# Turning memory rows with a VectorE block transpose, in a memory-augmented recurrent attention kernel

## The chip, the cores and the metric

The kernel runs on one core of one Trainium2 chip. That core has a matrix engine (TensorE, PE in the profile; its weight loads are listed apart as PEld), three engines for elementwise work (VectorE = DVE, ScalarE = ACT, GpSimd = POOL), a SyncE queue (SP) that issues most transfers, and 16 DMA engines that carry them. The metric is the device time of one execution in microseconds, the median over runs.

## The reference

A pre-normalised block with two halves. The first is attention with a recurrent memory: the 2048 tokens of 640 columns are cut into 64 segments of 32 tokens, and eight memory rows are carried from segment to segment.

```python
mem = mem0
for s in range(n_seg):                                # 64 segments, in order
    xs = x[:, s * seg_len:(s + 1) * seg_len, :].copy()
    h = jnp.concatenate([mem, xs], axis=1)            # 8 + 32 rows
    q = jnp.einsum('btd,dhe->bhte', h, Wq)            # 640 -> 32 heads x 128
    k = jnp.einsum('btd,dhe->bhte', h, Wk)
    v = jnp.einsum('btd,dhe->bhte', h, Wv)
    scores = jnp.einsum('bhqe,bhke->bhqk', q, k) * scale
    scores = jnp.where(mask[None, None], scores, -1000000000.0)
    p = _softmax(scores, axis=-1)
    o = jnp.einsum('bhqk,bhke->bhqe', p, v)
    o = jnp.einsum('bhte,hed->btd', o, Wo)            # back to 640 columns
    mem = o[:, :M, :].copy()                          # first 8 rows: next memory
    outs.append(o[:, M:, :])
```

Here x is the layer-normalised input. Its result is added to the input, normalised again and sent through a feed-forward half (640 to 1728, squared ReLU, back to 640, with biases), which is added once more. All tensors are bf16.

## The kernel before

The four attention weights (5 MB each) are loaded once and stay in SBUF. `wq`, `wk` and `wv` are tiles of 128 partitions with five blocks of 4096 columns: block c holds model columns 128c to 128c+127 on the partitions (`load_w`, L117 to L120, five transfers of 1 MB for each weight, issued on SP). In program order SP gets the first input rows, `wv`, `wq`, `wk`, then `wo` (`load_wo`, L142) and after that the smaller transfers of the steps. `start` (L669) computes the values, queries and keys of the first segment block by block as the weights land, and puts projections of later tokens between.

Then 64 calls of `step` (L380) run, one for each segment. Segments are handled in groups of four (b is the group, sp the place in it). The activations lie turned, model column on the partition, in `hT4[:, c, sp, 0:32]`: slots 0 to 7 hold the memory rows, the others the segment's first 24 tokens (filled ahead, by layer norm L171 and TensorE transposes L180). The last eight tokens of each segment are projected ahead for four segments together (`tail_units`). All projections go through `proj` (L206): for each block c and each of four column groups one matmul with 32 stationary columns and 512 moving columns.

A step projects q, k and v (L206), forms scores and softmax of the memory rows, applies them to the values, multiplies by Wo in `wo_rounds` (L238) and ends as follows. `wo_rounds` leaves in `pw` four groups of 32 partitions: two halves of the heads times two halves `ch` of the 640 output columns. `wo_out` (L241 to L247) copies the upper 64 partitions out with ScalarE (L245) and adds them to the lower 64 with VectorE (L246): the sum `o` has 64 partitions of 320 columns. `mem_to_hT` (L312) turns its memory rows with twenty small matmuls against an identity (L316) into PSUM tile `pm`, and VectorE copies that into `hT4` (L318). Only then can the next step's first projection load its weights, since those are the columns of `hT4`. In the halves `ch`, columns are interleaved in runs of 64 (`wov2`, L229), so that these matmuls can put each column on its partition.

The program order is the order on each engine; nothing reorders it. TensorE gets other work between the last `wo_rounds` matmul and the turn: up to six units of `fill` (L563), each of four to eight matmuls of later tokens' projections or Wo products, and what is left of `fill` after the turn (L567), ahead of the next projection. After the turn VectorE does layer norm work (`mid`, L566) and two transposes (L569, L575).

Results go to a DRAM tile `o_all`, in two stores for each step (`store_main`, L341) and two for each group's tails (L299). The values of tail tokens pass through DRAM as well: `vt_d` is written on L279 and read back by `tails_v_in` (L331), four transfers of 64 KB for each group. Their source is a view with j (four) outermost, then k (eight), then a run of 2 KB; the target is 32 partitions (L335, L338). At the end the feed-forward half runs in four tiles of 512 tokens; it loads `o_all` and the input and adds them in `prep_sum` (L635), which undoes the interleaving.

Of the kernel before, what the change touches and what calls it, by code (L numbers as in the profile page):

```python
# [9 lines left out]
ALU = mybir.AluOpType  # L10
AX = mybir.AxisListType
F32 = mybir.dt.float32
BF16 = mybir.dt.bfloat16
# [3 lines left out]
def kernel(  # L17
# [26 lines left out]
    DH = D // 2  # L44
    NB = S // 128
    NS = S // SEG
    HD = 24
# [28 lines left out]
    wo = wts.tile([128, H, D], BF16)  # L76

    ident = const.tile([128, 128], BF16)
    o_ring = [const.tile([128, DH], BF16, name="o%d" % k) for k in range(5)]
    o0 = o_ring[-1]  # L80
    nc.vector.memset(o0[0:64], 0.0)
    make_identity(nc, ident[:])
    mhalf = const.tile([128, 1], F32)
    nc.vector.memset(mhalf[:], -0.5)
# [22 lines left out]
    for o in o_ring:  # L107
        nc.gpsimd.memset(o[64:128], 0.0)

    ctx.enter_context(tc.manual_schedule(engines=None))  # L110

    def head(p):
# [3 lines left out]

    def load_w(w, src):  # L117
        w2d = src.rearrange("d h e -> d (h e)")
        for c in range(DC):
            nc.sync.dma_start(out=w[:, c * HE:(c + 1) * HE], in_=w2d[c * 128:(c + 1) * 128, :])  # L120

    xts = {}

# [9 lines left out]
        xts["t", g] = xt  # L133

    load_x(0)
    for ch in range(2):
        nc.scalar.dma_start(out=o0[32 * ch:32 * ch + M, :].rearrange("m (c f) -> m c f", f=64),
                            in_=A_mem0[0].rearrange("m (c t f) -> t m c f", t=2, f=64)[ch])
    load_tail_rows(0)
    load_w(wv, A_Wv)  # L140

# [25 lines left out]
    def ln_norm(b):  # L167
        mv, rs = xns[b]
        xn = s1.tile([128, D], BF16, tag="xn", name="xn")
        xt = xts.pop(b)  # L170
        nc.vector.tensor_scalar(out=xn[:], in0=xt[:], scalar1=mv[:, 0:1], scalar2=rs[:, 0:1],  # L171
                                op0=ALU.subtract, op1=ALU.mult)
        xns[b] = xn

    def ln_transpose(b):
# [65 lines left out]
    def wo_out(pw):  # L241
        o = o_ring[0]
        o_ring.append(o_ring.pop(0))
        tmp = s1.tile([128, DH], F32, tag="tk", name="otmp")
        nc.scalar.copy(out=tmp[0:64], in_=pw[64:128, 0:DH])  # L245
        nc.vector.tensor_tensor(out=o[0:64], in0=pw[0:64, 0:DH], in1=tmp[0:64], op=ALU.add)  # L246
        return o  # L247

    fill, late, mid, win = [], [], [], []
# [43 lines left out]
    def wo_tail_units(b):  # L293
        st = {}

        def out():
            o = wo_out(st["ps"])
            dst = o_all[:].rearrange("(b s t) d -> b s t d", s=4, t=SEG)
            for ch in range(2):  # L299
                nc.sync.dma_start(out=dst[b, :, HD:SEG, ch * DH:(ch + 1) * DH], in_=o[32 * ch:32 * ch + 32, :])  # L300

        def unit(k):
            def f():
                if k == 0:
                    st["ps"] = mmtile()
                wo_rounds(lambda p: oTts[b % 2][:, p, :], st["ps"], k * 16 // 10, (k + 1) * 16 // 10)
                if k == 9:
                    late.append(out)
            return f
        return [unit(k) for k in range(10)]  # L310

    def mem_to_hT(o, hT4, sp):  # L312
        pm = chn.tile([128, 512], F32, tag="ch", name="pm")
        for c in range(DC):
            for q in range(4):
                nc.tensor.matmul(pm[32 * q:32 * q + 32, c * M:(c + 1) * M], lhsT=o[:, (2 * c + q % 2) * 32:(2 * c + q % 2 + 1) * 32],  # L316
                                 rhs=ident[:, q // 2 * 32:q // 2 * 32 + M], start=True, stop=True)
        nc.vector.tensor_copy(out=hT4[:, :, sp, 0:M], in_=pm[:, 0:DC * M].rearrange("p (c m) -> p c m", m=M))  # L318

    def tails_in(b, sp, which="qk", h0=0, h1=H):  # L320
        q, k = [tails[b][w][:].rearrange("p h (k s) -> p h s k", s=4)[:, h0:h1, sp, :] if w in which else None for w in "qk"]
# [16 lines left out]
            eng.dma_start(out=vt4s[b][32 * g:32 * g + 32].rearrange("p s u e -> p (s u e)")[:, f0:f1], in_=src[g, :, :, f0:f1])  # L338

    def store_main(o, s):  # L340
        for ch in range(2):  # L341
# [392 lines left out]
    for b in range(NB):  # L734
        for sp in range(4):
# [40 lines left out]
            e = b * 4 + sp - (NS - 7)  # L776
# [30 lines left out]
    for t in range(S // NT):  # L807
# [6 lines left out]
        for fc in range(FC):  # L814
            ps = mmtile()
            for c in range(DC):
                if fc < FFULL:
                    nc.tensor.matmul(ps[:], lhsT=w1[:, c, fc * 128:(fc + 1) * 128], rhs=hnT[:, c, :],  # L818
                                     start=(c == 0), stop=(c == DC - 1))
                    continue  # L820
                for hh in range(2):
                    nc.tensor.matmul(ps[FREM * hh:FREM * (hh + 1), 0:HT], lhsT=w1[:, c, fc * 128:F],
                                     rhs=hnT[:, c, HT * hh:HT * (hh + 1)], start=(c == 0), stop=(c == DC - 1))
            w = NT if fc < FFULL else HT
# [3 lines left out]
            if more and fc >= 1 and (fc - 1) // 3 < NK4:  # L828
                k, stage = divmod(fc - 1, 3)
# [10 lines left out]
        for q in range(NK4):  # L840
# [6 lines left out]
            for hh in range(2):  # L847
                k = pr + 2 * hh
# [3 lines left out]
                if more and q and (hh == 0 or q == 1):  # L852
                    k = q if hh == 0 and q > 1 else hh
# [45 lines left out]
```

## Time and profile before

| | |
|---|---|
| median of 3 runs | 1021.12 us (1020.16 to 1023.35) |
| the profiled execution | 1020.98 us, span 1018.8 us |
| PE busy | 972.1 us (95%) |
| DVE busy | 621.6 us (61%) |
| ACT busy | 533.8 us (52%) |
| POOL busy | 309.3 us (30%) |
| HBM read, written | 38.37 MB, 9.44 MB |
| mean granted TensorE clock | 0.996 |

The span runs from the first to the last instruction; the execution's time is 2.2 us longer. An engine's busy time is the union of its instructions, so overlapping ones count once. Idle time is put down to whatever the engine waited for last. The share of the DMA engines is a mean over all 16: at 1.00 all carry packets, and packets that overlap on one engine can take it slightly over.

### The profile page before, as it was taken

The page shows a single profiled execution, that of the slowest core. Times are in us where ns is not written, and L with a number is a line of the kernel's source. Part 1 is how long each engine was busy: PE and PEld are TensorE (multiplying, and loading weights), DVE is VectorE, ACT ScalarE, POOL GpSimd, SP SyncE. Part 2 cuts the span into 40 slices and gives each one's busy share as a digit, 9 for nine tenths or more (in the row PEclk, how much of TensorE's full clock was granted, in tenths as well). Part 3 has the DMA queues.
Part 4 walks back from the last instruction along what each step waited for, and adds up shares of the span by engine and source line. Part 5 has one row for each costly group of instructions (what it writes and reads, how often), then busy time and mean ns, then how long its engine had stood idle before and what let it go on. Part 6 is the DMA issues. An engine that isn't in the chain of part 4 may idle for free.

```text
span 1018.8 us, 58958 instructions
## 1 busy us (share of the span) xinstructions
PE 972.1 (95%) x26951; PEld 582.4 (57%) x26960; DVE 621.6 (61%) x1740; ACT 533.8 (52%) x1229; POOL 309.3 (30%) x803
## 2 busy tenths in 40 slices
PE   5789899999999999999999999999999998999998
PEld 2345555655655755656655666556566565555565
DVE  2256676767666667566667666666666676466432
ACT  3335555565555555555555555555555555533431
POOL 2023333333333333323333332323232343433210
PEclk9999999999999999999999999999999999999999
DMA  9960101000101010000000000000000110612200
GB/s 362 398 190 21 23 7 30 8 24 7 35 7 30 7 38 11 27 10 27 15 21 16 24 19 15 22 14 28 15 22 8 48 35 6 212 48 66 78 26 26
DMA packets 39112, 51.57 MB, mean 51 GB/s; under 512 B 5968, under 2 KB 35024, under 8 KB 36944
## 3 DMA queue, kind: packets, MB, share of 16 engines
q1 hardware_dynamic: 38080, 47.48, 14.1%
q8 instruction: 210, 3.44, 1.4%
q10 hardware_dynamic: 784, 0.34, 0.1%
q14 instruction: 38, 0.31, 0.1%
HBM read 38.37 MB, written 9.44 MB: 47 GB/s over the span
## 4 chain that ended last, share of the span: by engine, by line
PE 88%; DMA 6%; DVE 2%; issue 1%; ACT 1%; SPq 0%; DVEq 0%; POOL 0%; ACTq 0%; POOLq 0%
PE ps L206 48%; PE pw L238 15%; PE y L850 6%; PE ps L818 5%; PE ps L238 3%; DMA wk<-in_A_Wk_dram 3%; PE po L449 2%; PE po L355 2%; PE sm L421 2%; DMA wq<-in_B_w_dram 1%; DMA xt<-in_A_x_dram 1%; PE ps L493 1%; PE pm L316 1%; PE ps L489 1%; DVE o L246 1%
## 5 line engine op out<-in xcount | busy, mean ns | idle before, releaser
L206 PEld LDWEIGHTS <-hT 128*32 128x32 bf16 x7680 | 200.9, 97 | 171.6 <-issue 14.2
L238 PE MATMUL pw<-wo,oT 128*32 128x320 bf16 x4224 | 184.1, 300 | 7.1 <-issue 5.4
L206 PE MATMUL ps<-wv,hT 128*32 128x512 bf16 x2520 | 170.5, 379 | 0.9 <-ACT v L502 0.7
L206 PE MATMUL ps<-wq,hT 128*32 128x512 bf16 x2520 | 160.2, 381 | 5.3 <-DVE hT L318 5.3
L206 PE MATMUL ps<-wk,hT 128*32 128x512 bf16 x2520 | 159.5, 380 | 0.1
L238 PEld LDWEIGHTS <-oT 128*32 128x32 bf16 x4224 | 104.6, 96 | 60.5 <-ACT oT L215 13.6
L222 ACT ACTIVATE row<-ps 128x512 bf16<-128x512 f32 x156 | 93.3, 599 | 75.7 <-PE ps L206 75.1
L227 DVE STREAM_TRANSPOSE qT<-row 128x512 bf16<-128x512 bf16 x128 | 90.4, 707 | 65.8 <-ACT row L222 65.7
L548 POOL TENSOR_TENSOR pkt<-ek,rk 128x64 bf16<-128x64 bf16 x64 | 18.8, 294 | 352.5 <-DVE rk L546 352.5
L224 ACT CAST row<-ps 128x512 bf16<-128x512 f32 x115 | 68.0, 591 | 32.7 <-PE ps L206 32.5
L374 POOL COPY qz<-qT 128x96 bf16<-128x96 bf16 x126 | 33.4, 265 | 139.6 <-DVE qT L227 139.4
L325 POOL COPY kT<-kTt 128x1024 bf16<-128x1024 bf16 (+1 forms) x65 | 71.9, 1107 | 12.5 <-DVE kTt L227 12.5
L206 PEld LDWEIGHTS <-hTt 128*32 128x32 bf16 x1920 | 55.0, 97 | 32.3 <-issue 3.7
L245 ACT COPY otmp<-pw 64x320 f32<-64x320 f32 x66 | 27.9, 423 | 81.8 <-PE pw L238 81.8
L544 DVE TENSOR_REDUCE zk<-ek 128x8 f32<-128x320 bf16 x64 | 31.1, 486 | 63.5 <-ACT ek L542 63.5
L365 ACT CAST oT<-po 128x512 bf16<-128x512 f32 x128 | 68.7, 589 | 1.6
L246 DVE TENSOR_TENSOR o<-pw,otmp 64x320 bf16<-64x320 f32 x66 | 31.8, 482 | 61.6 <-ACT otmp L245 61.6
L227 DVE STREAM_TRANSPOSE kT<-row 128x512 bf16<-128x512 bf16 x65 | 46.1, 709 | 31.3 <-ACT row L224 31.3
L850 PE MATMUL y<-wq,wk 128*128 128x320 bf16 x416 | 60.9, 299 | 0.0
L405 ACT CAST row<-ps 128x256 bf16<-128x256 f32 x126 | 40.7, 375 | 31.2 <-PE ps L206 29.4
L521 ACT CAST v<-ps 128x512 bf16<-128x512 f32 x63 | 36.9, 586 | 30.7 <-PE ps L206 30.7
L502 ACT CAST v<-ps 128x512 bf16<-128x512 f32 x63 | 36.9, 586 | 30.0 <-PE ps L206 30.0
(113 smaller groups left out, 1633.6 us busy)
## 6 DMA issues: line engine op xcount, KB each, us to landing
wv<-in_A_Wv_dram SPq DMA_DIRECT2D x5, 1024.0 KB
wq<-in_A_Wq_dram SPq DMA_DIRECT2D x5, 1024.0 KB
wk<-in_A_Wk_dram SPq DMA_DIRECT2D x5, 1024.0 KB
vt<-vt_d SPq DMA_DIRECT2D x60, 64.0 KB
xt<-in_A_x_dram SPq DMA_DIRECT2D x20, 160.0 KB
vt_d<-row SPq DMA_DIRECT2D x22, 128.0 KB
wo<-in_A_Wo_dram SPq DMA_DIRECT2D x2, 1280.0 KB
wo<-in_A_Wo_dram SPq DMA_DIRECT2D x4, 640.0 KB
```

The source lines that it names most:

```text
L206: nc.tensor.matmul(ps[32 * k:32 * k + 32, :], lhsT=lhs(c), rhs=wr[:, c, n, k], start=(c == 0), stop=(c == DC - 1))
L222: nc.scalar.mul(out=row, in_=ps, mul=scale)
L224: nc.scalar.copy(out=row, in_=ps)
L227: nc.vector.transpose(out=dst[:, n * 16:(n + 1) * 16, 0:32], in_=row.rearrange("p (h e) -> p h e", e=32))
L238: nc.tensor.matmul(pw[32 * j:32 * j + 32, 0:DH], lhsT=lhs(p), rhs=wov2[:, head(p), ch], start=(h == 0), stop=(h == 15))
L246: nc.vector.tensor_tensor(out=o[0:64], in0=pw[0:64, 0:DH], in1=tmp[0:64], op=ALU.add)
L325: nc.gpsimd.tensor_copy(out=kT[:, h0:h1, SEG:2 * SEG].rearrange("p h (j k) -> p h j k", k=TL), in_=k.unsqueeze(2).to_broadcast([128, h1 - ...
L365: nc.scalar.copy(out=oTg[:, n, :, :, M:NK], in_=po[:, :, n * 128:(n + 1) * 128].rearrange("p g (j q) -> p g j q", q=32))
L405: nc.scalar.copy(out=row[:, u * 256:(u + 1) * 256], in_=ps[:, u * 256:(u + 1) * 256])
L502: nc.scalar.copy(out=v[:, 0:512], in_=ps0[:])
L818: nc.tensor.matmul(ps[:], lhsT=w1[:, c, fc * 128:(fc + 1) * 128], rhs=hnT[:, c, :], start=(c == 0), stop=(c == DC - 1))
L850: nc.tensor.matmul(y[:, hh, 0:DH], lhsT=f1T[:, fc, k * 128:(k + 1) * 128], rhs=w2[:, fc, cs], start=(fc == 0), stop=False, skip_group_chec ...
```

## The change

The eight memory rows are turned by one VectorE instruction that transposes each 32x32 block of a 128x160 tile, and one VectorE copy into `hT4`. The twenty matmuls and the PSUM tile `pm` go. For that, `o` becomes 128 partitions of 160 columns: partition group q (of 32) holds model columns 160q to 160q+159. A block transpose then leaves model column 160q + 32c + f on partition 32q + f of block c. So block c of the turned activations holds four runs of 32 model columns, 160 apart, instead of 128 consecutive ones.

Everything that shares this contraction follows: the three weights are loaded with rows in that order (`load_w`: the source of each 1 MB transfer is four runs of 32 rows), the layer norm writes its columns in that order, and the Wo columns are interleaved in runs of 160. `wo_out` makes `o` in two copies and two adds of 64x160 instead of one of each of 64x320. Every store of `o` becomes four transfers of 160 columns instead of two of 320, and so does the load of the first memory rows. `prep_sum` adds plainly, and the clearing of the `o` tiles' upper halves goes.

```diff
     def load_w(w, src):
         w2d = src.rearrange("d h e -> d (h e)")
+        rows = w2d.rearrange("(q c f) e -> c q f e", q=4, c=DC)
         for c in range(DC):
-            nc.sync.dma_start(out=w[:, c * HE:(c + 1) * HE], in_=w2d[c * 128:(c + 1) * 128, :])
+            nc.sync.dma_start(out=w[:, c * HE:(c + 1) * HE], in_=rows[c])
...
-    for ch in range(2):
-        nc.scalar.dma_start(out=o0[32 * ch:32 * ch + M, :].rearrange("m (c f) -> m c f", f=64),
-                            in_=A_mem0[0].rearrange("m (c t f) -> t m c f", t=2, f=64)[ch])
+    for q in range(4):
+        nc.scalar.dma_start(out=o0[32 * q:32 * q + M, :], in_=A_mem0[0][:, q * DQ:(q + 1) * DQ])
...
-        nc.vector.tensor_scalar(out=xn[:], in0=xt[:], scalar1=mv[:, 0:1], scalar2=rs[:, 0:1],
-                                op0=ALU.subtract, op1=ALU.mult)
+        nc.vector.tensor_scalar(out=xn[:].rearrange("p (c q f) -> p c q f", c=DC, q=4),
+                                in0=xt[:].rearrange("p (q c f) -> p c q f", c=DC, q=4),
+                                scalar1=mv[:, 0:1], scalar2=rs[:, 0:1], op0=ALU.subtract, op1=ALU.mult)
...
-    wov2 = wo[:].rearrange("p h (c t f) -> p h t c f", t=2, f=64)
+    wov2 = wo[:].rearrange("p h (a t f) -> p h t a f", a=2, t=2)
...
-        tmp = s1.tile([128, DH], F32, tag="tk", name="otmp")
-        nc.scalar.copy(out=tmp[0:64], in_=pw[64:128, 0:DH])
-        nc.vector.tensor_tensor(out=o[0:64], in0=pw[0:64, 0:DH], in1=tmp[0:64], op=ALU.add)
+        tmp = s1.tile([128, DH], F32, tag="otmp", name="otmp")
+        for a in range(2):
+            nc.scalar.copy(out=tmp[0:64, a * DQ:(a + 1) * DQ], in_=pw[64:128, a * DQ:(a + 1) * DQ])
+        for a in range(2):
+            nc.vector.tensor_tensor(out=o[64 * a:64 * a + 64], in0=pw[0:64, a * DQ:(a + 1) * DQ],
+                                    in1=tmp[0:64, a * DQ:(a + 1) * DQ], op=ALU.add)
...
     def mem_to_hT(o, hT4, sp):
-        pm = chn.tile([128, 512], F32, tag="ch", name="pm")
-        for c in range(DC):
-            for q in range(4):
-                nc.tensor.matmul(pm[32 * q:32 * q + 32, c * M:(c + 1) * M], lhsT=o[:, (2 * c + q % 2) * 32:(2 * c + q % 2 + 1) * 32],
-                                 rhs=ident[:, q // 2 * 32:q // 2 * 32 + M], start=True, stop=True)
-        nc.vector.tensor_copy(out=hT4[:, :, sp, 0:M], in_=pm[:, 0:DC * M].rearrange("p (c m) -> p c m", m=M))
+        mt = s1.tile([128, DC, 32], BF16, tag="mt", name="mt")
+        nc.vector.transpose(out=mt[:], in_=o[:].rearrange("p (c f) -> p c f", f=32))
+        nc.vector.tensor_copy(out=hT4[:, :, sp, 0:M], in_=mt[:, :, 0:M])
...
     def store_main(o, s):
-        for ch in range(2):
-            nc.sync.dma_start(out=o_all[s * SEG:s * SEG + HD, ch * DH:(ch + 1) * DH],
-                              in_=o[32 * ch + M:32 * ch + 32, :])
+        for q in range(4):
+            nc.sync.dma_start(out=o_all[s * SEG:s * SEG + HD, q * DQ:(q + 1) * DQ],
+                              in_=o[32 * q + M:32 * q + 32, :])
...
     def prep_sum(t, k, got):
         ot, fx = got
-        fv = fx.rearrange("p (c t f) -> p t c f", t=2, f=64)
-        nc.vector.tensor_tensor(out=fv, in0=ot.rearrange("p (t c f) -> p t c f", t=2, f=64), in1=fv, op=ALU.add)
+        nc.vector.tensor_tensor(out=fx, in0=ot, in1=fx, op=ALU.add)
         return fx
```

More of the change, by code (lines that the diff above doesn't have):

```diff
@@ L44 @@
     DH = D // 2
+    DQ = D // 4
     NB = S // 128
@@ L78 @@
     ident = const.tile([128, 128], BF16)
-    o_ring = [const.tile([128, DH], BF16, name="o%d" % k) for k in range(5)]
+    o_ring = [const.tile([128, DQ], BF16, name="o%d" % k) for k in range(5)]
     o0 = o_ring[-1]
-    nc.vector.memset(o0[0:64], 0.0)
+    nc.vector.memset(o0[:], 0.0)
     make_identity(nc, ident[:])
@@ L105 @@
     oTts = [const.tile([128, H, 32], BF16, name="oTt%d" % k) for k in range(2)]
-    for o in o_ring:
-        nc.gpsimd.memset(o[64:128], 0.0)
     ctx.enter_context(tc.manual_schedule(engines=None))
@@ L298, in out @@
             dst = o_all[:].rearrange("(b s t) d -> b s t d", s=4, t=SEG)
-            for ch in range(2):
-                nc.sync.dma_start(out=dst[b, :, HD:SEG, ch * DH:(ch + 1) * DH], in_=o[32 * ch:32 * ch + 32, :])
+            for q in range(4):
+                nc.sync.dma_start(out=dst[b, :, HD:SEG, q * DQ:(q + 1) * DQ], in_=o[32 * q:32 * q + 32, :])
         def unit(k):
@@ L340, in store_main @@
     def store_main(o, s):
-        for ch in range(2):
-            nc.sync.dma_start(out=o_all[s * SEG:s * SEG + HD, ch * DH:(ch + 1) * DH],
-                              in_=o[32 * ch + M:32 * ch + 32, :])
+        for q in range(4):
+            nc.sync.dma_start(out=o_all[s * SEG:s * SEG + HD, q * DQ:(q + 1) * DQ],
+                              in_=o[32 * q + M:32 * q + 32, :])
     oTg = oT[:].rearrange("p (n g j) q -> p n g j q", n=2, g=G)
```

## The prediction

> **What bounds the kernel now.** I read the page first: busy shares and the chain that ended last.
>
> ```profile
> PE 972.1 (95%) x26951; PEld 582.4 (57%) x26960; DVE 621.6 (61%) x1740; ACT 533.8 (52%) x1229; POOL 309.3 (30%) x803
> ...
> DMA  9960101000101010000000000000000110612200
> ...
> PE 88%; DMA 6%; DVE 2%; issue 1%; ACT 1%; SPq 0%; DVEq 0%; POOL 0%; ACTq 0%; POOLq 0%
> ```
>
> TensorE carries the chain, except for the first slices (25 us each), where the DMA engines are full. The chain in order of time, narrowed to the first 70 us, shows what they do:
>
> ```profile
> 5.74 12.33 DMA xt<-in_A_x_dram
> 18.09 16.74 DMA wk<-in_A_Wk_dram
> 34.85 10.19 DMA wk<-in_A_Wk_dram
> ...
> 45.08 1.92 PE pa L206 x16
> ...
> 61.61 0.35 PE pm L316 x20
> ```
>
> Until 45.04 us the end is set by weight transfers; the last `wk` block frees TensorE at 45.08. So there are two regimes: a load of 45 us bound by transfers, and steps bound by TensorE. For a step I took the timeline of one with full `fill` (columns: start, duration):
>
> ```profile
> 452.49 0.42 ACT L245 COPY otmp<-pw 64x320 f32<-64x320 f32 x1 [1.11 <-PE pw L238]
> 452.95 0.48 DVE L246 TENSOR_TENSOR o<-pw,otmp 64x320 bf16<-64x320 f32 x1 [0.80 <-ACT otmp L245]
> 453.50 0.28 PE L316 MATMUL pm<-ident,o 128*32 128x8 bf16 x20
> 453.63 0.82 PE L206 MATMUL ps<-wk,hTt 128*32 128x512 bf16 x12
> 453.90 0.20 DVE L318 CAST hT<-pm 128x40 bf16<-128x40 f32 x1 [0.47 <-PE pm L316]
> 454.15 0.67 PEld L206 LDWEIGHTS <-hT 128*32 128x32 bf16 x16 [0.19 <-DVE hT L318]
> 454.28 0.82 PE L206 MATMUL ps<-wq,hT 128*32 128x512 bf16 x12
> ```
>
> The twenty turning matmuls hold TensorE for 0.13 us (453.50 to 453.63). The turned rows are ready at 454.10, their weights load at 454.15, the projection starts at 454.28. The waits say how often that is late:
>
> ```profile
> PE ps L206 <- DVE hT L318: 5.3, 15, 0.4
> ```
>
> In 15 steps TensorE stands still for the turned rows, 0.35 us each; in the other 47 `fill` covers them.
>
> Last, the transfers by stretch, with the share of 16 DMA engines and GB/s as the last two columns:
>
> ```profile
> 8.00:40.00 32.00, 25.08 (x418) 12.24 (x422) 4.70 (x10) 12.38 (x21) 2.10 (x8) 1.00 1.02 414
> 168.90:169.70 0.80, 0.80 (x22) 0.42 (x16) 0.33 (x1) 0.44 (x1) 0.80 (x4) 1.00 0.76 202
> 483.30:486.00 2.70, 2.70 (x89) 2.31 (x84) 2.23 (x6) 1.56 (x6) 0.58 (x4) 1.00 0.25 77
> 742.00:745.00 3.00, 3.00 (x96) 1.69 (x92) 2.24 (x6) 1.90 (x6) 1.16 (x5) 1.00 0.25 78
> ```
>
> The first is the weight load: all engines. The second is `load_tail_rows` (source 16 by 8 rows), well spread. The last two are `tails_v_in`, whose source has an outermost axis of four: a quarter of the engines. Four such transfers are in flight together there and still fill only a quarter, so they queue on the same four engines.
>
> **The weight load.** It moves 15 transfers of 1024 KB, 15.73 MB. Before: 15.73 MB / 414 GB/s = 38.0 us. After, each source reads four by 32 rows of 8 KB: outermost axis four, the form of `tails_v_in`. From those rows I expect four of 16 engines for every transfer, the same four each time. One engine carried 414/16 = 25.9 GB/s with these 8 KB rows; four carry 103.5, and 15.73 MB take 152.0 us: +114.0. The nearest rows bound it. Not at all (0) if the form spreads as `load_tail_rows` does; 15.73 MB / 77 GB/s = 204 us (+166) if the rate of the 2 KB rows holds. I take 114, since the packets stay those of the weight load. Nothing covers it: TensorE already waits for these transfers, `start` needs every block in order, and the work that it holds (39 us busy between 4 and 58) is no longer than the load was. Behind the weights in the SP queue are `wo`, the next input rows and `vt`. `wo` spreads over 16 engines, but its part on those four queues behind `wk`, so it ends about as long after the last `wk` block as before (bounds: -1.2 us, the stall at 58.38 that would go, to 0).
>
> [...]
>
> **Off TensorE.** 64 times 20 matmuls and their weight loads go. In the 47 covered steps that is 0.13 us each, -6.1 us, if the turned rows come in time; they are needed by 454.15 then (454.28 less 0.13).
>
> **The new chain in a step**, on the clock of the timeline above. ScalarE: 128x256 takes 375 ns and 128x512 589, so 0.836 ns an element; 160 elements take about 295, and the second of a back-to-back pair begins some 0.19 later. Copies 452.49 to 452.98 (before 452.91). Adds: PSUM reads of 128x40 and 128x128 take 200 and 292 ns, 1.05 ns an element, so 160 elements save 167 of 483: 316. The first runs 452.82 to 453.13, the second ends about 453.40 (before 453.43). Transpose of 128x160: between the rows for 128x64 (245) and 128x256 (424), by line 335: 453.44 to 453.77. Copy of 128x40: 200 as the PSUM row at most, to 454.01; weights from 454.06. That is 0.09 before need, so the covered steps keep their gain, and the 15 others gain about 0.06 each: -0.9. Together -7.0 us.
> Bounds: durations that do not shrink with halves (copies 0.42 after each other, adds 0.48, transpose 0.42) give 454.54: 47 x 0.31 + 15 x 0.5 = +22. Halved ones (0.21, 0.24, transpose 0.245, copy 0.14) give -6.1 and 15 x 0.38 = -5.7 more: -12. I take -7, by the rows on both sides of each size.
>
> **Beside other work.** DVE gets some 0.5 us more a step, ACT 0.07, in steps of 13 us at 61% and 52%: what follows L318 (`mid`, L569, L575) is needed in the next step only; 0. SP issues 128 plus 32 stores more at 0.35 and 0.61 us; it waits 634.7 us on L342 for `o`, which covers them; behind it stand `vt` loads that are read a group later; 0. Layer norm with runs of 32: 20 instructions of 574 ns, at most 668 (the 128x512 row of L827, 534, scaled to 640): 2 us on DVE in idle time; 0. Wo matmuls with runs of 160: same 320 columns, as L850 with unbroken columns takes 299 and L238 300; 0. `prep_sum` unbroken: 16 of about 500 ns beside the feed-forward matmuls; -3 to 0, I take 0. Two more loads of the first memory rows on ACT (1.4 and 0.7 us an issue) and the five clears off POOL lie beside the first weight block, which now lands later; 0. No wait is added on a queue other than DVE's own order.
>
> **Sum**, against the profiled execution: 1020.98 + 114.0 - 7.0 = 1128.0 us. The median is 0.14 above that execution, so the same number holds for it.
>
> **Rivals.** (1) The loads spread: either the form reaches all engines, as 16 by 8 rows do, or each transfer takes another four. Then the load stays at 38 us and only the steps change: 1020.98 - 7 = 1014, faster. For it: 32 rows a piece are more than the eight of `vt`. Against it: a share of 0.25 with four transfers queued. It decides as soon as more than four engines work: at eight the load is 76 us and the time 1052. (2) The chain is late: the vector work doesn't shrink with size, `fill` runs out in every step, +22 instead of -7: 1157. For it: fixed costs show in every short row (245 ns for 64 columns). Against: the pairs of L405 overlap. (3) Four engines at the slower rate of 2 KB rows, with some of it, say half, made up: +140, 1154. Against: packets of 8 KB remain.
>
> **How the numbers follow.** Four shared engines with the chain in time: 0.75, 1128, own range 1118 to 1140. Rival 2: 0.07. Rival 3: 0.08. Rival 1: 0.10, of which 0.09 end at 1014 and 0.01 between. The range, 1116 to 1155, leaves out rival 1 and the far ends of 2 and 3. No change here means within 0.3%, about 3 us, which is what a measurement of this kernel can tell. Faster 0.09, same 0.01, slower 0.90.
>
> **What would show it.** DMA share near 0.25 and about 104 GB/s through the first 155 us; the last wait for `wk` ending near 159 instead of 45; steps 0.1 us shorter on average with no L316; a transpose of about 0.33 us before L318's successor; L206 waiting for it no more than in 15 steps. A share near 1 in the first slices would overthrow the forecast; a wait for the turned rows in every step would be rival 2.

## The result, and the profile after

The changed kernel takes 1137.12 us (median of 4 runs, 1135.06 to 1139.67), against 1020.96 us for the kernel before: a ratio of 1.114, 95% interval 1.1116 to 1.1165. It is slower by 116 us. The forecast was 1128, with its own range 1118 to 1140, and the range over all cases 1116 to 1155. The profiled execution took 1136.06 us, its span 1134.3 us, with a mean granted TensorE clock of 0.956.

First the page of the changed kernel: busy shares, TensorE's granted clock, the DMA engines and their GB/s in slices of 28 us, and the chain that ended last.

```profile
PE 983.5 (87%) x25671; PEld 560.5 (49%) x25680; DVE 654.7 (58%) x1886; ACT 535.6 (47%) x1311; POOL 304.3 (27%) x798
...
PEclk9965659999999999999999999999999999999999
DMA  2222354000000101010001001010000010242200
GB/s 92 109 113 106 123 174 147 16 16 13 22 14 16 28 11 28 8 37 14 20 14 26 25 9 32 8 28 14 25 14 21 24 39 20 84 141 70 71 24 24
...
PE 11%; DVE 1%; issue 0%; ACT 0%; DVEq 0%
```

Where the row of the DMA engines began with `99`, it begins with four slices of `2`, at 92 to 113 GB/s: the weight load now fills the first six slices. TensorE's clock reads 0.5 to 0.7 in the third to sixth of them. The chain of this run can't be used: followed back it breaks off in the feed-forward half, and its shares add up to 12%.

The windows of the changed kernel over the load show the same by stretch (last two columns: share of the 16 DMA engines, GB/s).

```profile
8.00:60.00 52.00, 9.29 (x81) 3.62 (x85) 1.60 (x5) 1.55 (x2) 0.00 (x0) 1.00 0.26 104
60.00:110.00 50.00, 21.67 (x205) 8.23 (x200) 1.13 (x3) 6.97 (x12) 0.79 (x2) 0.58 0.27 110
110.00:165.00 55.00, 15.78 (x164) 6.19 (x160) 2.49 (x4) 4.32 (x8) 1.36 (x6) 0.59 0.41 134
```

The clock of 1.00 in the first of these rows can't be relied on, nor the mean of 0.956 that includes it: the clock records of this trace begin at 64.6 us. Matmuls of 512 columns take 620 to 634 ns (medians by tile) from 8 to 60 us, much as they do from 68 to 112 us, where the clock is 0.50, and 379 ns from 171 to 230 us, where it is 1.00.

What TensorE waits for in the changed kernel (us in total, times, longest):

```profile
PE pa L205 <- DMA wv<-in_A_Wv_dram: 39.4, 5, 8.3
PE pa L205 <- DMA wk<-in_A_Wk_dram: 39.2, 5, 9.7
PE pa L205 <- DMA wq<-in_A_Wq_dram: 28.3, 5, 6.2
PE ps L205 <- DVE hT L317: 17.1, 15, 2.2
...
PE ps L816 <- DVE o L247: 4.1, 1, 4.1
```

All fifteen weight blocks are waited for, 106.9 us in total, where the kernel before waited 5.9 us (its rows are among the experiments). The wait for the turned rows has grown from 5.3 to 17.1 us, but the kernel before also waited for the same chain one instruction earlier, where its turning matmuls needed the adds. At the start of the feed-forward half the wait is 4.1 us, where it was 1.0. These rows of the kernel before are:

```profile
PE pm L316 <- DVE o L246: 6.3, 10, 1.1
...
PE ps L818 <- DVE o L246: 1.0, 1, 1.0
```

The ten waits of the first row fall in ten of the 15 steps, so the chain cost 11.6 us of waiting before and 17.1 us now.

I cut both profiled executions at the same matmuls. The last column says what the prediction had.

| stretch | before, us | after, us | difference | forecast |
|---|---|---|---|---|
| start to the last `wk` block's first matmul | 45.08 | 164.74 | +119.7 | +114.0 |
| to the last Wo matmul of step 0 | 15.45 | 15.00 | -0.4 | -1.2 to 0 |
| steps 1 to 5 | 66.2 | 67.9 | +1.7 | with the next row |
| steps 6 to 62 | 741.15 | 731.41 | -9.7 | -7.0 in all steps |
| last step and feed-forward half | 150.9 | 155.2 | +4.3 | -3 to 0, taken as 0 |
| span | 1018.8 | 1134.3 | +115.5 | +107.0 |

So the load carries the result, as forecast. The smaller rows come close in their sum, but, as the runs show, not for the reasons that I gave, and in part by luck. The timeline of the changed kernel shows this for the step that the prediction showed (step 30; start, duration):

```profile
568.38 0.48 ACT L245 COPY otmp<-pw 64x160 f32<-64x160 f32 x2 [1.00 <-PE pw L237]
...
568.89 0.67 DVE L247 TENSOR_TENSOR o<-pw,otmp 64x160 bf16<-64x160 f32 x2 [0.76 <-ACT otmp L245]
...
569.59 0.34 DVE L316 STREAM_TRANSPOSE mt<-o 128x160 bf16<-128x160 bf16 x1
...
569.97 0.18 DVE L317 COPY hT<-mt 128x40 bf16<-128x40 bf16 x1
...
570.20 0.34 PEld L205 LDWEIGHTS <-hT 128*32 128x32 bf16 x12 [0.42 <-DVE hT L317]
```

From the first copy to the weights' load it takes 1.82 us (568.38 to 570.20), where the kernel before took 1.66 (452.49 to 454.15) with its twenty matmuls in between.

### The profile page after: what moved, and what is told of

Read it like the earlier page. It is cut to its first block, busy times and chain, and to the rows that moved or that the text cites. A ratio compares the mean times of both kernels' runs of the same rounds, so it can differ in the third digit from the quotient of the medians.

```text
span 1134.3 us, 57176 instructions
## 1 busy us (share of the span) xinstructions
PE 983.5 (87%) x25671; PEld 560.5 (49%) x25680; DVE 654.7 (58%) x1886; ACT 535.6 (47%) x1311; POOL 304.3 (27%) x798
## 5 line engine op out<-in xcount | busy, mean ns | idle before, releaser
L205 PEld LDWEIGHTS <-hT 128*32 128x32 bf16 x7680 | 190.0, 97 | 306.9 <-issue 120.5
L237 PE MATMUL pw<-wo,oT 128*32 128x320 bf16 x4224 | 179.1, 300 | 2.5 <-DVE o L247 1.0
L205 PE MATMUL ps<-wq,hT 128*32 128x512 bf16 x2520 | 159.6, 382 | 17.2 <-DVE hT L317 17.1
L237 PEld LDWEIGHTS <-oT 128*32 128x32 bf16 x4224 | 101.1, 96 | 54.9 <-ACT oT L214 16.2
L205 PEld LDWEIGHTS <-hTt 128*32 128x32 bf16 x1920 | 57.3, 105 | 53.5 <-issue 21.5
L247 DVE TENSOR_TENSOR o<-pw,otmp 64x160 bf16<-64x160 f32 x132 | 41.9, 317 | 55.6 <-ACT otmp L245 53.6
L245 ACT COPY otmp<-pw 64x160 f32<-64x160 f32 x132 | 31.8, 288 | 69.9 <-PE pw L237 68.3
L824 ACT ACTIVATE wv<-ps,b1f 128x512 bf16<-128x512 f32 (+1 forms) x56 | 37.4, 672 | 31.0 <-PE ps L816 30.2
L501 ACT CAST v<-ps 128x512 bf16<-128x512 f32 x63 | 36.9, 585 | 30.7 <-PE ps L205 30.7
## 6 DMA issues: line engine op xcount, KB each, us to landing
vt_d<-row SPq DMA_DIRECT2D x22, 128.0 KB
```

The source lines that it names most:

```text
L205: nc.tensor.matmul(ps[32 * k:32 * k + 32, :], lhsT=lhs(c), rhs=wr[:, c, n, k], start=(c == 0), stop=(c == DC - 1))
L237: nc.tensor.matmul(pw[32 * j:32 * j + 32, 0:DH], lhsT=lhs(p), rhs=wov2[:, head(p), ch], start=(h == 0), stop=(h == 15))
L247: nc.vector.tensor_tensor(out=o[64 * a:64 * a + 64], in0=pw[0:64, a * DQ:(a + 1) * DQ], in1=tmp[0:64, a * DQ:(a + 1) * DQ], op=ALU.add)
L824: nc.scalar.activation(out=r[:, 0:w], in_=ps[:, 0:w], func=ACT.Relu, bias=b1f[:, fc:fc + 1], scale=1.0)
```

## The experiments

Ratios are to the kernel before on the same chip; its median was 1015.94 to 1021.76 us on the chips used. Times without an interval come from a single run.

**The block transpose without the reordered load.** The original load and layer norm; the Wo columns and the first memory rows are interleaved in runs of 32 instead, and the feed-forward's sum undoes that.

```diff
-        rows = w2d.rearrange("(q c f) e -> c q f e", q=4, c=DC)
...
-            nc.sync.dma_start(out=w[:, c * HE:(c + 1) * HE], in_=rows[c])
+            nc.sync.dma_start(out=w[:, c * HE:(c + 1) * HE], in_=w2d[c * 128:(c + 1) * 128, :])
...
-    wov2 = wo[:].rearrange("p h (a t f) -> p h t a f", a=2, t=2)
+    wov2 = wo[:].rearrange("p h (c a t f) -> p h t a c f", a=2, t=2, f=32)
```

> The block transpose alone: the order of the model columns, the weight load and the layer norm are those of before; instead the Wo columns are interleaved in runs of 32, so that partition group q of o holds columns 128c + 32q + f, and prep_sum undoes it. Theory A: the load of before, and of the change only the steps: the trace of the changed kernel has steps 6 to 62 shorter by 9.7 us together, the feed-forward half longer by 4.5, so about 1021 - 9.7 + 4.5 = 1016 us. The recorded forecast for the steps alone was 1014. Rival (the second add starts only when the first has ended, so turned rows come later than TensorE needs them): L206's successor waits for them in most steps, gain of the covered steps nearly nothing, 1016 to 1021. Second rival (runs of 32 columns slow the Wo matmuls): these rise above 300 ns and the time above 1021.

Measured: 1017.46 us against 1018.24, ratio 0.9989 (0.9974 to 1.0004). The last `wk` block starts at 44.77 us, and the load in the window from 8 to 30 us is back at 415 GB/s. From this kernel to the changed one are 119.7 us by medians. So the whole loss is the load's, and the block transpose alone cannot be told from no change. Its time lies in the range of the first rival, and its trace has the late chain: 17.0 us of waiting for the turned rows in 15 steps.

**The weight load, cut in other ways.** Five kernels, all in the window from 8 to 30 us. First the changed kernel with each 1 MB transfer issued as four of 32 rows:

```diff
-            nc.sync.dma_start(out=w[:, c * HE:(c + 1) * HE], in_=rows[c])
+            for q in range(4):
+                nc.sync.dma_start(out=w[32 * q:32 * q + 32, c * HE:(c + 1) * HE], in_=rows[c][q])
```

> The changed kernel with each 1 MB weight transfer issued as four of 32 rows (256 KB), one for each run; same rows, same order, same bytes. Theory A (a transfer whose source has an outermost axis of four uses four DMA engines, the same ones each time): the first slices go back to a DMA share near 1.0, the last wait for wk ends at 45 to 50 us instead of 164.7, and the time falls by 115 to 120 us, to 1016 to 1024 us. Theory B (the order of the rows, or their distance in HBM, makes the load slow): the load stays near 160 us and the time near 1137.

Then the kernel before with a source of eight runs of 16 rows, and of sixteen runs of 8 (`q=16`):

```diff
+        rows = w2d.rearrange("(q c f) e -> c q f e", q=8, c=DC)
...
-            nc.sync.dma_start(out=w[:, c * HE:(c + 1) * HE], in_=w2d[c * 128:(c + 1) * 128, :])
+            nc.sync.dma_start(out=w[:, c * HE:(c + 1) * HE], in_=rows[c])
```

> The kernel before, with the source of each weight transfer as 8 runs of 16 rows (the weights' rows land in another order, so it computes another product of the same size). Theory A: eight engines, a block every 5.1 us, the load ends near 84 us, time 1021 + 39 = 1060. Theory B (short or distant runs): runs half as long as the change's, so at least as slow a load as with four, 1135 or more.

> As the run with 8, with 16 runs of 8 rows (again another order of rows, a product of the same size). Theory A: all 16 engines, no loss, 1021 within 3 us. Theory B: the shortest runs, the slowest load.

These left a second slowdown to explain, so two more on the kernel before: rows in their old order, but 32 partitions at a time; and all 128 partitions at a time, but every fifth row of HBM.

```diff
+            for q in range(4):
+                nc.sync.dma_start(out=w[32 * q:32 * q + 32, c * HE:(c + 1) * HE],
+                                  in_=w2d[c * 128 + 32 * q:c * 128 + 32 * q + 32, :])
```

> The kernel before, with each weight transfer issued as four of 32 consecutive rows into 32 partitions each: HBM is read in the same unbroken order as before, only the partitions that the 16 engines write at one time change. The split load of the changed order had all engines busy and half the rate (222 GB/s), so a second cause is open. Theory C (writing to 32 partitions at a time is what halves the rate): near 222 GB/s here too, the last wk wait ends near 80 us, time 1018 + 37 = 1055. Rival D (the distance of the runs in HBM halves it): the rate of before, 414 GB/s, time within 5 us of the kernel before.

```diff
+        rows = w2d.rearrange("(r c) e -> c r e", c=DC)
...
+            nc.sync.dma_start(out=w[:, c * HE:(c + 1) * HE], in_=rows[c])
```

> The kernel before, with block c of each weight taken from every fifth row of 8 KB: one transfer of 128 rows into 128 partitions as before, source rows 40 KB apart (another order of the weights' rows, a product of the same size). Theory C: the target is that of before, so the load is that of before and the time within 5 us of it. Rival D: broken reading of HBM, a slower load, +20 us or more.

Measured (the packet is the median time of an 8 KB packet in the window, counted in the traces' DMA records; times are medians where more than one run was made):

| kernel | share of engines | GB/s | packet, ns | last `wk` block, us | time, us |
|---|---|---|---|---|---|
| before | 1.01 | 411 | 309 | 45.1 | 1020.96 |
| changed: four runs of 32 | 0.25 | 97 | 313 | 164.7 | 1137.12 |
| four transfers of 32 rows | 1.03 | 222 | 612 | 81.7 | 1055.88 |
| eight runs of 16 | 0.52 | 130 | 593 | 120.7 | 1091.45 |
| sixteen runs of 8 | 1.02 | 235 | 603 | 74.0 | 1045.5 |
| old order, 32 partitions at a time | 1.03 | 218 | 622 | 83.6 | 1054.38 |
| every fifth row, 128 partitions | 1.02 | 415 | 309 | 45.0 | 1016.35 |

The two windows that separate the causes of the second slowdown, 32 partitions at a time and then strided rows:

```profile
8.00:30.00 22.00, 9.65 (x101) 3.07 (x105) 1.04 (x4) 1.59 (x2) 0.00 (x0) 1.00 1.03 218
```

```profile
8.00:30.00 22.00, 16.88 (x266) 7.80 (x270) 2.10 (x6) 8.04 (x13) 0.79 (x2) 1.00 1.02 415
```

Two things follow. First, in these runs the share of the engines goes with the source's outermost runs: 4, 8 and 16 runs gave shares of 0.25, 0.52 and 1.02. (The traces do not name the engines; a share of 0.25 with packets as long as before is read as four at work.) Second, engines at work are not enough: in four of these forms the packets take twice as long (593 to 622 ns against 309). Scattered source rows are not the reason, since strided rows load at 415 GB/s; consecutive rows written into 32 partitions at a time load at 218. The split load therefore repairs the count of engines, and still loses 3.65% (ratio 1.0365, 1.0323 to 1.0408).

Why the two loads into 32 partitions at a time, in transfers of 256 KB, run at half the rate (222 and 218 GB/s against 411) is not shown. Nor do these runs explain that four engines are not slowed (313 ns) while eight are (593 ns): which partitions the engines write at one time is not in the traces.

**The twenty matmuls put back.** The next kernels start from the block transpose with the original load. This one adds, ahead of it, twenty matmuls of the size and number that the kernel before had, with the wait on the adds that comes with their PSUM buffer; nothing reads their result.

```diff
     def mem_to_hT(o, hT4, sp):
+        pm = chn.tile([128, 512], F32, tag="ch", name="pm")
+        for c in range(DC):
+            for q in range(4):
+                nc.tensor.matmul(pm[32 * q:32 * q + 32, c * M:(c + 1) * M], lhsT=ident[:, 32 * q:32 * q + 32],
+                                 rhs=ident[:, 0:M], start=True, stop=True)
```

> The in-order kernel with the block transpose, and the twenty small matmuls back on TensorE at their old place, against the identity and into a tile that nobody reads: TensorE's work of before with the new vector chain. Theory A (the steps gained because TensorE has less to do): steps 6 to 62 go from 731.2 us back towards 741.2, time +6 to +10 us over the in-order kernel. Rival (the gain of the covered steps is only what their wait leaves, and most of the gain is stalls of TensorE that show no releaser, which follow the wait and not the number of instructions): +0 to +2 us.

Measured: 1040.17 us against 1015.94, ratio 1.0222 (1.0195 to 1.0249). By the profiled spans it is 22.8 us above the same kernel without them (1038.1 and 1015.3), more than either theory allowed. The waits of TensorE in it, and then in the kernel before:

```profile
PE pm L317 <- DVE o L246: 10.4, 12, 1.4
PE pw L236 <- issue: 3.7, 6, 1.7
...
PE po L452 <- issue: 2.4, 7, 0.5
```

```profile
PE pa L206 <- DMA wk<-in_A_Wk_dram: 2.7, 2, 1.7
...
PE pa L206 <- DMA wq<-in_A_Wq_dram: 1.6, 3, 0.6
PE pa L206 <- DMA wv<-in_A_Wv_dram: 1.6, 1, 1.6
...
PE pw L238 <- issue: 5.4, 15, 1.2
...
PE po L449 <- issue: 1.4, 4, 0.5
```

Both have pauses before Wo products and softmax-value products for which the profile knows no releaser ("issue"). The block transpose alone has nearly none:

```profile
PE po L447 <- issue: 1.0, 3, 0.6
...
PE pw L236 <- issue: 0.2, 1, 0.2
```

So I cut steps 6 to 62 of each profiled run in two. The turn runs from the end of a step's last Wo matmul to the start of the first query projection with the new memory rows, the rest from there to the end of the next last Wo matmul. I also counted, in the DMA records, how often TensorE left more than 0.28 us between two matmul starts, ending 1.2 to 1.75 us after a 16 KB packet of the instruction queue had landed, the waits for the turned rows and the matmuls into `pm` left out.

| kernel | turn, us | rest, us | such pauses |
|---|---|---|---|
| before | 115.5 | 625.6 | 23 |
| changed kernel | 114.4 | 617.0 | 4 |
| block transpose, original load | 114.6 | 616.7 | 5 |
| with twenty matmuls again | 128.0 | 624.8 | 22 |
| with five (below) | 139.6 | 624.3 | 21 |
| with one (below) | 122.5 | 628.6 | 24 |
| one add (below) | 107.9 | 617.3 | 5 |

The turn of the changed kernel is hardly shorter than before. The gain lies in the rest, where nothing was edited, and it comes and goes with the matmuls into `pm`. The other traces show how far one trace can be trusted here. Four more have the steps of the kernel before (the loads of eight and sixteen runs, of 32 partitions at a time and of every fifth row): their rest is 621.8 to 623.9 us with 14 to 21 pauses, so the kernel before stands at the upper end. The split load and the kernel with two adds and the earlier loads (below) have the steps of the changed kernel: 615.9 and 616.9 us with 6 and 4 pauses. So the gain in the rest is 5 to 10 us, not a firm 8.6.

The count itself could be chance in part: packets land some 3.9 us apart, so a window of 0.55 us would hold about one pause in seven. In the kernel before it holds 23 of the 30 pauses over 0.28 us, in the changed kernel 4 of 10.

In the turn the twenty cost 13.4 us: in the 35 covered steps they hold `fill` back by 0.27 us each.

**Fewer instructions, or fewer matmuls.** Two kernels asked what of the twenty brings the pauses back. Five matmuls of 128x128 in place of the twenty:

```diff
+        for c in range(5):
+            nc.tensor.matmul(pm[:, 0:128], lhsT=ident[:], rhs=ident[:, 0:128], start=True, stop=True)
```

> The block transpose alone, with five matmuls of 128x128 against the identity (into a tile that nothing reads) in each step where the run before had twenty small ones. Both take the same place in TensorE's order, the same wait for the second add, and about the same time in TensorE (20 matmuls 0.27 us; 5 of 128 columns some 5 x 0.054 = 0.27 us), but five bring 10 instructions into TensorE's queue in a step and twenty bring 40. Theory F (instruction fetch): a part of what twenty cost are the pauses of TensorE that end 1.3 to 1.6 us after a packet of the instruction queue has landed: in steps 6 to 62 22 of them with twenty matmuls (10.0 us from start to start), 5 without (2.4). With five they should be near 5, and the time that of the block transpose alone plus the 14 us that the wait and the matmuls themselves take: 1030 to 1034. Rival P (place): the pauses come from the wait, or from the work that is pushed behind it, whatever the number of instructions; then about 22 pauses stay, and the time is 1038 to 1042.

And one small matmul:

```diff
+        nc.tensor.matmul(pm[0:32, 0:M], lhsT=ident[:, 0:32], rhs=ident[:, 0:M], start=True, stop=True)
```

> The block transpose alone, with one matmul of 32x8 against the identity (into a tile that nothing reads) in each step, in the place and with the wait for the second add that the twenty had. In a step with cover (step 30 of the run with twenty) the fill work behind it started 0.38 us later: 0.12 us for the wait and 0.27 us for the matmuls; with one it should start about 0.15 us later, of which the wait of 0.11 us for the rows takes up most, so the matmul itself costs 0 to 0.1 us in each of 57 steps, 0 to 6 us. Theory W (the wait): the pauses that follow an instruction fetch come back (about 21 in steps 6 to 62, 9.6 us from start to start, against 5 and 2.4) because TensorE's queue is held at this place, whatever stands there; the time is 1023 to 1029. Rival T (time taken): they come because the matmuls push the rest of the step back; with one nothing is pushed, 4 to 8 pauses stay, and the time is 1017 to 1021.

Measured: 1050.58 us against 1017.92 with five, ratio 1.0332 (1.0316 to 1.0348); 1038.53 us against 1021.76 with one, ratio 1.0166 (1.0141 to 1.0191). The waits with one matmul:

```profile
PE pm L315 <- DVE o L246: 10.1, 12, 1.4
...
PE po L449 <- issue: 4.1, 10, 0.6
...
PE pw L236 <- issue: 1.6, 4, 0.6
```

Theory F fell: 10 instructions a step in place of 40 leave 21 pauses. Its price was also wrong; five large matmuls lengthen the turn by 25 us, almost twice what the twenty small ones did. Theory W holds for the pauses: one matmul, 2 instructions, brings back 24. Its time is above both forecasts, because I had put the turn's cost at 0 to 6 us (it is 8) and the pauses' at 7 (the rest grew by 12). What is shown: a matmul into `pm` at this place, of each of the three sizes tried, costs 8 to 12 us in the rest of 57 steps, and doing without it is where the block transpose gains in the steps. Each of them also waits for the adds (12 waits, 10.1 to 10.5 us in total), because `pm` and `pw` share one PSUM buffer; no run has the matmul without that wait, so which of the two brings the pauses is not shown. That the pauses hang on instruction fetch is a coincidence in time, not shown either; why they come back stays open.

**One add instead of two.** The products of one half of the heads are put at another column of `pw`, so that two copies cross over and one add covers 128 partitions.

```diff
-                    nc.tensor.matmul(pw[32 * j:32 * j + 32, 0:DH], lhsT=lhs(p), rhs=wov2[:, head(p), ch],
+                    nc.tensor.matmul(pw[32 * j:32 * j + 32, DQ * (1 - kh):DQ * (1 - kh) + DH], lhsT=lhs(p), rhs=wov2[:, head(p), ch],
...
-        for a in range(2):
-            nc.scalar.copy(out=tmp[0:64, a * DQ:(a + 1) * DQ], in_=pw[64:128, a * DQ:(a + 1) * DQ])
-        for a in range(2):
-            nc.vector.tensor_tensor(out=o[64 * a:64 * a + 64], in0=pw[0:64, a * DQ:(a + 1) * DQ],
-                                    in1=tmp[0:64, a * DQ:(a + 1) * DQ], op=ALU.add)
+        nc.scalar.copy(out=tmp[0:64], in_=pw[64:128, 0:DQ])
+        nc.scalar.copy(out=tmp[64:128], in_=pw[0:64, 2 * DQ:3 * DQ])
+        nc.vector.tensor_tensor(out=o[:], in0=pw[:, DQ:2 * DQ], in1=tmp[:], op=ALU.add)
```

> The in-order kernel with one add of 128x160 in place of two of 64x160: the Wo products of the two head halves go to columns 160 to 479 and 0 to 319 of pw, two ScalarE copies bring what is missing across, and one add makes all 128 partitions. If the serial second add is what makes the turned rows late: rows ready about 0.35 us sooner, the covered steps gain 0.1 to 0.15 us each and the others 0.35, some 10 us, 1007. If TensorE's stalls without a releaser return once it no longer waits for the rows: 4 to 5 us of that are lost, 1012. If the chain is not the limit: no change, 1017.

Measured: 1009.87 us against 1015.94, ratio 0.9930 (0.9905 to 0.9956), between the forecasts of 1007 and 1012; the pauses stayed at 5. Its timeline of step 30:

```profile
445.84 0.29 ACT L243 COPY otmp<-pw 64x160 f32<-64x160 f32 x1 [1.00 <-PE pw L236]
...
446.46 0.32 DVE L245 TENSOR_TENSOR o<-pw,otmp 128x160 bf16<-128x160 f32 x1 [0.86 <-ACT otmp L244]
...
446.82 0.35 DVE L313 STREAM_TRANSPOSE mt<-o 128x160 bf16<-128x160 bf16 x1
...
447.43 0.46 PEld L204 LDWEIGHTS <-hT 128*32 128x32 bf16 x12 [0.19 <-DVE hT L314]
```

From the first copy to the weights' load it now takes 1.59 us instead of 1.82. The turn falls by 6.7 us, to 107.9: the covered steps get the 0.13 us that the prediction promised (median turn 1.90 us before, 1.87 in the changed kernel, 1.77 here), and the uncovered ones are no longer late (1.73, 1.93, 1.69).

**The feed-forward half.** With four stores a step it is longer by 4 to 5 us (155.2 us in the changed kernel and 156.0 in the block transpose alone, against 150.9). All seven traces with four stores and the loads in their old place lie at 154.6 to 156.4 us, the five with two stores at 150.9 to 152.1. The changed kernel's SP queue shows eight stores of two steps ahead of the loads for the second tile, over 7.92 us; in the kernel before there were four, over 3.41 us (its row comes first).

```profile
881.84 3.41 SPq L342 DMA_DIRECT2D o_all<-o  x4
```

```profile
994.72 7.92 SPq L341 DMA_DIRECT2D o_all<-o  x8
1002.74 0.35 SPq L630 DMA_DIRECT2D wk<-o_all  x1
1003.19 0.38 SPq L631 DMA_DIRECT2D wk<-in_A_x_dram  x1
```

On VectorE the sum of those loads comes late, and the adds of the last step stand behind it (the changed kernel again):

```profile
1005.58 0.49 DVE L636 TENSOR_TENSOR wk<-wk 128x640 bf16<-128x640 bf16 x1 [5.73 <-DMA wk<-in_A_x_dram]
...
1007.42 0.66 DVE L247 TENSOR_TENSOR o<-pw,otmp 64x160 bf16<-64x160 f32 x2
```

To test it, the loads are issued ahead of the last-but-one step's output, with two adds and with one:

```diff
+    first = {k: prep_load(1, k) for k in range(NK4)}
     end_output(NS - 2)
...
-                got[k] = prep_load(t + 1, k)
+                got[k] = first[k] if t == 0 else prep_load(t + 1, k)
```

> The block transpose alone (original weight load), with the loads of the second feed-forward tile issued ahead of the last-but-one step's output instead of at the loop over the tiles. Theory S (stores): the feed-forward's 5.0 us more than before (139.95 against 134.96 from the end of the last-but-one step's last Wo product set) come from the eight stores of a step, where there were four, that stand on SP ahead of these loads, and from VectorE's adds that queue behind a wait for them; then the 3.9 us gap of TensorE at the feed-forward's start goes and the time is 1012.5 to 1014.5. Rival V: the gap is VectorE's own, with the adds, the transpose and the copy of the last two steps in its queue, and the loads have no part; then the gap and 1017.5 stay.

> The version with one 128x160 add, with the loads of the second feed-forward tile issued ahead of the last-but-one step's output. By theory S the 3.3 us gap at the feed-forward's start goes and the time is 1005.5 to 1007.5 (one add alone: 1009.9); by rival V it stays at 1009.9.

Measured: 1014.42 us against 1017.92, ratio 0.9968 (0.9956 to 0.9980), with two adds; 1005.75 us against 1017.92, ratio 0.9890 (0.9870 to 0.9911), with one. From step 62's last Wo matmul to the end it takes 152.3 and 151.4 us, where the kernels without the edit took 156.0 and 155.4. TensorE's wait at the half's start, with two adds and then with one:

```profile
PE ps L817 <- DVE o L246: 1.8, 1, 1.8
```

```profile
PE ps L815 <- DVE o L245: 1.1, 1, 1.1
```

These were 3.9 and 3.3 us. Theory S holds: the half is back at about the length that it has with two stores, and of the waits that are left, 1.0 us stood in the kernel before as well. By medians the gain is less sure: with two adds the interval just meets that of the same kernel without the edit (0.9974 to 1.0004), and so it does with one (0.9905 to 0.9956). The last kernel has the lowest median of all, 1.1% below the kernel before.

## Why the prediction was right, and where not

**The load: right in its mechanism, 5% too small.** By the share, four of sixteen engines carried it: it is 0.25 to 0.27, and the rate 104 GB/s until 60 us, where the forecast had 103.5. The forecast's reading of the `tails_v_in` rows, an outermost axis of four and a share of 0.25, fits all three counts of runs tried: 0.25, 0.52 and 1.02 with 4, 8 and 16. The term came to 119.7 us instead of 114.0. Of the 5.7 us, 4 are the last three `wk` blocks, which came 11.2 to 11.6 us apart instead of the 10.1 us of the blocks before. The `wo` transfers, issued at 130 and 137 us, run beside them (share 0.41 in the last window); the prediction saw `wo` queue behind `wk`, not slow it. The stretch behind the load came out at -0.4 us, within its bounds.

**Rival 1, that the loads spread,** is out in both its forms by the share. Its price was wrong too: the prediction said that eight engines would mean 1052 us and sixteen 1014. Eight gave 1091, and sixteen 1045 to 1056, since the packets take twice as long in these forms (593 to 622 ns against 309). **Rival 3** is out by 104 GB/s with packets of 313 ns.

**The steps: the sum nearly right, the reason wrong.** Forecast -7.0 us, measured -9.7 in steps 6 to 62 and +1.7 in steps 1 to 5, so -8.0. That this comes so near is in part luck: steps 1 to 62 took 807.4 us in the trace of the kernel before and 801.4 to 802.4 in the four others with its steps, against 798.5 to 800.0 with the block transpose and two adds. Against those four the gain is 1 to 4 us. Of the -9.7 only -1.1 lie in the turn. The step that failed is in the chain: "The first runs 452.82 to 453.13", that is, the first add starts 0.33 us after the first copy. It started 0.51 us after it, right behind the second copy. In the trace the first copy raises no semaphore; the second raises the one that the first add waits for, and the second add waits for neither copy. Both copies write the tile `otmp`; that this is why they share one signal is argued, not tested. The second add then began only when the first had ended, where I had let them overlap by 0.05 us. The durations themselves were right: copies 288 ns (295 forecast), adds 317 (316), transpose 345 (335), copy of the rows 181 (200 at most). So the weights loaded 0.16 us later than before, where the prediction had them 0.09 ahead of need. Of steps 6 to 62, 35 covered ones gained 0.02 us each instead of 0.13, the 14 with the longest turn 0.13, and the 8 with the shortest, which have no cover, lost 0.20 instead of gaining 0.06 (medians). Two separate tiles for the two copies were not tried; one add for both halves makes up for the same wait. The prediction also took the cost of the uncovered steps too low, at 0.35 us each in 15 steps: in ten of them the wait for the adds, 6.3 us in total, stood ahead of it.

What lies outside the turn, -8.6 us in these two traces, was no term of the sum. I counted the twenty matmuls as 0.13 us of TensorE's time. What they cost beyond that is pauses elsewhere in the step, and the experiments show that these go with the matmuls and come back with a single one. **Rival 2** (chain late, +22) had the direction of the chain's error; its cost stayed small, since `fill` covers all but 15 steps.

**What was costed at nothing and was not nothing: the doubled stores.** The prediction said that SP's wait for `o` covers them. That holds within the steps, where SP still waits 562.7 us for `o`, but not where loads that are needed soon stand behind them on SP. In the feed-forward half this cost some 4 us. Step 4 took 2.0 us longer than before: GpSimd waited 4.06 us for a bias row ahead of its copies of the queries, and TensorE stood 2.03 us for those. The load of that row stands behind the stores on SP; that this is why it came late is read from the order there, and no run tested it.

Step 5 took 1.9 us longer for another reason. It has a wait of 1.92 us for the turned rows; the block transpose with the original load has one of 1.93 us there and takes 12.7 us for the step, the changed kernel 14.4. Behind the wait the changed kernel's clock fell, as its windows show (PE busy first, the granted clock third from the end); the two with 0.57 and 0.72 hold a stretch at 0.50 from 235.3 to 238.7 us:

```profile
233.00:235.00 2.00, 0.23 (x7) 0.00 (x0) 1.05 (x4) 1.55 (x4) 0.74 (x3) 1.00 0.03 9
235.00:237.00 2.00, 1.84 (x20) 0.80 (x24) 1.55 (x6) 0.00 (x0) 2.00 (x5) 0.57 0.10 23
237.00:240.00 3.00, 3.00 (x44) 1.32 (x40) 0.80 (x2) 1.18 (x2) 1.33 (x5) 0.72 0.18 48
```

In the 3.4 us before 235.3 us TensorE was busy for 1.46 us. The other kernel's trace has 1.47 us busy from 114.6 to 118.0 us, around its own wait, and the full clock after it. Why the clock fell in one and not in the other is open. The kernel before had such a stretch at 0.50 too, from 61.9 to 65.3 us in its step 1, which took 14.2 us where the changed kernel's took 12.9. Steps 1 to 3 were shorter by 2.2 us together, which is why steps 1 to 5 come to +1.7 and not to +3.9.

In the steps of these two traces, the chain's error and the pauses that went about cancel, so the forecast of 1128 is 9 us low by the load (5.7) and the feed-forward half (4.3).

## What to carry to other kernels

When rows are to be regrouped, look first at what the outermost axis of the load becomes: here it moved the end of the weight load from 45 to 165 us, while the same regrouping on the other side, in the columns of Wo, cost nothing that could be measured (its matmuls took 300 ns before and after). A small matmul that had to wait inside a filled TensorE queue cost more here than its time (one of 32x8 in each step about 18 us over the kernel), and replacing the twenty by vector work shortened the rest of steps 6 to 62 by 5 to 10 us although the turn got hardly shorter (114.4 us against 115.5); in all, the block transpose alone did not change the time measurably (ratio 0.9989). Two copies into one tile raised one signal here, after the second, so the reader of the first half waited for both (it started 0.51 us after the first copy); one instruction over both halves gained 0.6%. More, smaller stores cost 4 to 5 us here in the feed-forward half, where a load that was needed soon stood behind them on the same queue.

## What the runs showed of the hardware that I had not expected

- Sixteen busy DMA engines moved 218 to 235 GB/s or 411 to 415, with the same 8 KB packets and the same share of about 1.02; the packets took 603 to 622 ns or 309. Source rows five apart cost nothing (415 GB/s against 411). So the share alone did not tell at what rate a load ran.
- One matmul of 32x8, placed into TensorE's queue behind a wait in each step, cost about 18 us over the kernel (ratio 1.0166 against 0.9989 without it); in steps 6 to 62 of the profiled run 8 us where it stands, and 12 us later in the steps.
- Pauses of TensorE that end 1.2 to 1.75 us after a packet of the instruction queue has landed: 14 to 24 in steps 6 to 62 of the eight traces with a matmul at that place, and 4 to 7 in the six without one. Their number did not grow when a step had 10 or 40 instructions more in place of 2 (24, 21 and 22).
- TensorE's clock stood at 0.50 for 3.4 us, from 235.3 to 238.7 us in the changed kernel, after 3.4 us in which the engine was busy for 1.46 us.
